# Stating every engine's instruction order for the attention and the first part of the first MLP

## The chip, the cores and the metric

The kernel runs on one core of one Trainium2 chip. The metric is device time in microseconds (us), the median of several runs; the output must agree with a float32 reference. The kernel is one program without loops at run time: every instruction of every engine is written out, and each engine works through its own list in order.

## What is computed

Attention with a causal mask and a linear memory term, for 4 batches, 8 heads, 576 positions and 64 values per head, then an MLP with squared ReLU (512 to 2048 to 512), then one with a softmax-weighted unit and a layer norm (512 to 1024 to 512), on 2304 tokens.

```
scores = scale * q @ k.T ; scores = where(causal, -1e9, scores)
a = exp(scores - max) ; a /= sum(a) + 1e-9 ; local = a @ v
q_p = elu(q) + 1 ; mem_out = (q_p @ M_prev) / (q_p . z_prev + 1e-6)
x = g * mem_out + (1 - g) * local          # g = sigmoid(beta), by head
r = max(x @ w_in, 0) ; y = (s * r * r + b) @ w_out
h = y @ w2_in ; solu = h * softmax(h) ; out = (layernorm(solu) * g_ln) @ w2_out
```

## The kernel before

**Units.** Attention goes through 16 units: 4 batches by 4 pairs of heads. The queries of a unit are cut into four chunks of 128 (index 0 to 3) and a tail of 64 for both heads (index 4). In the names of the rows the first number is the unit: s4_2 are the scores of unit 4, chunk 2; pr4_2_0 the probabilities of that chunk, head 0.

**A unit's chain.** `scores` (L329) multiplies on TensorE into ps_s, one pair of PSUM banks with a single buffer: one bank per head. Four groups follow each other there: chunks 0 and 1 together, 2, 3, and the tail (`tail_scores`, L360). VectorE adds the mask and takes the row maximum (L345, L363 for the tail), which also empties the banks for the next group. ScalarE takes the exponential (L312). TensorE transposes the result (L386, tiles pp), ScalarE copies it out of PSUM (L390, tiles pt), and `values` multiplies it by v (L421, and L424 for the tail, tiles po and pe). The memory term has its own transposes (L302 and L306) and products (L426, L427); the reciprocal sums are transposed at L292; VectorE writes the unit's result to xb (L428, L429).

**Matmul shapes.** The scores contract over 64 rows and two heads stand one above the other in the array; the row's form is 64\*128. The value products fill 64 columns each, two heads side by side; their form is 128\*64. All other matmuls use the whole array, 128\*128. In the trace each of these narrow float32 matmuls stands as two records, so x12 of L329 are six matmuls of the program.

**Filler.** `first_part` runs the first 4 of 16 column blocks of the first MLP on finished tokens between the attention's own matmuls (h: L440 to L442, y: L502 to L504), with its split of x (L469, L470) and its nonlinearity (L443, L450, L451, L454). `decode` turns float64 weights into two float32 parts: a load into one of three buffers raw (L154), then ScalarE (L159, L186) and VectorE (L160, L162, L164, L165, L187).

**What sets the order.** A scheduler of the framework puts the instructions of each engine in order when the program is built, from the order of the source and a timeline model of its own. The source steers it where it says that one instruction is to be issued after another: `exps` and `hidden` leave a mark, and `decode_to` (L197 to L202) asks that a decode step be issued after the last mark. The flag `attended` turns true once attention has been issued.

Of the kernel before, what the change touches and what calls it, by code (L numbers as in the profile page):

```python
# [17 lines left out]
P = 128  # L18
NEG = -8.0e9
FMAX = 3.0e38  # L20


@with_exitstack
def attention_mlp_kernel(
# [10 lines left out]
    B, NPAIR, _, NCH, _, D = q.shape  # L35
# [81 lines left out]
    order = [("in", f) for f in range(FP1)] + [("out", f) for f in range(FP1)]  # L117
# [50 lines left out]
    def decode(n):  # L168
        key = order[n]
        sc = None  # L170
        if key[0] == "in2" and key[2] >= 3:

            k = key[2]
            if k == 3:
                blk[3] = fetch(n)[0]
            d, x, y = ((0, 3, 0), (3, 2, 3), (2, 2, 0), (1, 1, 2))[k - 3]
            a = blk[d]
            nc.gpsimd.tensor_tensor(a, blk[x], blk[y], ALU.subtract)
        else:
            a, sc = fetch(n)  # L180
            if key[0] == "in2":
                blk[key[2]] = a
        pool = wpools[in_b(n)]
        w = pool.tile([P, 2, WN], F32R, tag="w", name=f"w{n}")
        if sc is None:
            nc.scalar.activation(w[:, 0], a, AF.Copy)  # L186
            nc.vector.tensor_tensor(w[:, 1], a, w[:, 0].bitcast(F32), ALU.subtract)  # L187
        else:
            nc.scalar.activation(w[:, 0], a, AF.Copy, scale=sc)
            nc.vector.scalar_tensor_tensor(w[:, 1], a, sc, w[:, 0].bitcast(F32), ALU.mult, ALU.subtract)  # L190
        wtiles[key] = w
# [4 lines left out]
    mark = [None]  # L196

    def decode_to(n):
        while decoded[0] < min(n, NW):
            with tc.issue_after(mark[0]) if mark[0] else nullcontext():  # L200
                decode(decoded[0])
            decoded[0] += 1  # L202

# [7 lines left out]
    class Attention:  # L211
# [102 lines left out]
        def scores(self, u, *cs):  # L314
# [23 lines left out]
            for i in cs:  # L338
                n = (i + 1) * P
                prs, mxs = [], []  # L340
                for j in range(2):
# [4 lines left out]
                                                   big[:, CF * P - i * P:CF * P - i * P + n],  # L346
                                                   -scale, FMAX, ALU.add, ALU.min, mx)
                    prs.append(pr)
# [3 lines left out]
        def tail_scores(self, u, ss):  # L352
# [5 lines left out]
            for t in range(2):  # L358
                cols = slice(t * HS, (t + 1) * HS)
                nc.tensor.matmul(ss[:, t, 0:HS], raw[:, QT:RL], raw[:, cols], start=True, stop=True)  # L360
                m0 = FMAX if t == 0 else mx
                mx = self.tiny.tile([P, 1], F32, tag="mx", name="mx")
# [71 lines left out]
    attended = [False]  # L434
# [39 lines left out]
    def first_part(k, pools):  # L474
# [13 lines left out]
        for f in range(FP1):  # L488
            h = ps[0].tile([P, 512], F32, tag="mh"[len(ps) - 1], name=f"h{k}_{f}")
            r, g = gtiles(f"{k}_{f}")  # L490
            decode_to(f + 1)
            hidden(wtiles["in", f], xh, xl, n, h[:, 0:n], r[:, 0:n], g[:, 0, 0:n], g[:, 1, 0:n])
            gq.append(g)
            yield
        for c in range(NC):
            pt = ps[-1].tile([P, 512], F32, tag="m", name=f"y{k}_{c}")
            o = pt[:, 0:n]
            decode_to(2 * FP1)
            for f in range(FP1):
                wc = [wtiles["out", f][:, t, c * P:(c + 1) * P] for t in range(2)]  # L500
                gh, gl = (gq[f][:, t, 0:n] for t in range(2))
                nc.tensor.matmul(o, wc[0], gh, start=(f == 0), stop=False)  # L502
                nc.tensor.matmul(o, wc[1], gh, start=False, stop=False)  # L503
                nc.tensor.matmul(o, wc[0], gl, start=False, stop=(f == FP1 - 1))  # L504
            y = ys.tile([P, NB], F32, tag="y", name=f"yo{k}_{c}")
            nc.scalar.activation(y[:, 0:n], o, AF.Copy)
            nc.sync.dma_start(yd[:, c, t0:t0 + n], y[:, 0:n])
            yield
# [27 lines left out]
    with ExitStack() as fctx:  # L536
# [7 lines left out]
        with ExitStack() as actx:  # L544
# [15 lines left out]
            for g in range(G + LAG):  # L560
                u, i = divmod(g, NS)
# [14 lines left out]
                if 0 <= g - LAG:  # L576
# [6 lines left out]
                    if li == CF:  # L583
                        at.values(lu)
                        at.load(lu + 2, "v")
                        if lu % NPAIR == NPAIR - 1:
                            filler.append(first_part(lu // NPAIR, fpools))
                decode_to(min(int(g / 3.4), RA))
                if filler and g >= FG:
                    debt += (B - 1) * (FP1 + NC) / (G - FG)  # L590
# [84 lines left out]
    def mlp2(mctx):  # L675
# [32 lines left out]
        def products(q, mxs):  # L708
# [6 lines left out]
            def product(o, form, k, more):  # L715
                yh, yl = form
                for i in range(KH):
                    w = wtiles["in2", i, k]
                    nc.tensor.matmul(o, yh[:, i], w[:, 0], start=(i == 0 and not more), stop=False,
                                     skip_group_check=True)  # L720
                    nc.tensor.matmul(o, yh[:, i], w[:, 1], start=False, stop=False, skip_group_check=True)
                    nc.tensor.matmul(o, yl[:, i], w[:, 0], start=False, stop=(i == KH - 1), skip_group_check=True)

            def leave(t, half, o, x, m0, m):
                nc.vector.tensor_tensor_reduce(hn[t][:, half * WN:(half + 1) * WN], o, x, -1.0, m0,
                                               ALU.add, ALU.min, m)
# [7 lines left out]
            product(W, fs1, 3, False)  # L734
            leave(1, 1, W, u3, FMAX, mxs[2])
            product(X, fa12, 1, True)
            leave(0, 0, X, big[:, 0:WN], FMAX, mxs[0])
            product(W, fs4, 2, True)
# [55 lines left out]

    with ExitStack() as mctx:
        mlp2(mctx)


_INS = ["z_prev", "beta", "moe_w_in", "moe_w_out", "moe_s", "moe_b", "moe2_w_in", "moe2_w_out", "moe2_g_ln"]
# [50 lines left out]
```

## Time and profile before

| what | us |
|---|---|
| median of 3 runs (849.80 to 850.04) | 849.98 |
| profiled execution, whole time | 849.68 |
| its span, first to last instruction | 847.5 |
| TensorE matmuls busy (PE) | 828.6 |
| TensorE weight loads busy (PEld) | 660.1 |
| VectorE busy (DVE) | 541.5 |
| ScalarE busy (ACT) | 550.6 |

The attention's last matmul starts at 305.5 us; the rest of the first MLP ends near 641 us, the second MLP fills the remainder. The granted TensorE clock is full (1.00, so the 2.4 GHz level) in all but the last stretch. Times are from the start of the span. A busy PE means that some matmul is in flight by the profile's model of their ends; a group's real price is the distance from its start to the start of the next group.

### The profile page before, as it was taken

The page shows a single profiled execution, that of the slowest core. Times are in us where ns is not written, and L with a number is a line of the kernel's source. Part 1 is how long each engine was busy: PE and PEld are TensorE (multiplying, and loading weights), DVE is VectorE, ACT ScalarE, POOL GpSimd, SP SyncE. Part 2 cuts the span into 40 slices and gives each one's busy share as a digit, 9 for nine tenths or more (in the row PEclk, how much of TensorE's full clock was granted, in tenths as well). Part 3 has the DMA queues.
Part 4 walks back from the last instruction along what each step waited for, and adds up shares of the span by engine and source line. Part 5 has one row for each costly group of instructions (what it writes and reads, how often), then busy time and mean ns, then how long its engine had stood idle before and what let it go on. Part 6 is the DMA issues. An engine that isn't in the chain of part 4 may idle for free.

```text
span 847.5 us, 13346 instructions
## 1 busy us (share of the span) xinstructions
PE 828.6 (98%) x4930; PEld 660.1 (78%) x4930; DVE 541.5 (64%) x1305; ACT 550.6 (65%) x1134; POOL 117.3 (14%) x124
## 2 busy tenths in 40 slices
PE   8999999999999999999999999999999999999997
PEld 6666776777677678888889888888887888888885
DVE  4989776968884747544556444473689666666552
ACT  5988787867876856665677666576785544444432
POOL 3122021101120200000000020020103333322000
PEclk9999999999999999999999999999999999999999
DMA  8344343534453013561223121121120000000001
GB/s 255 122 138 147 129 153 109 174 121 135 141 188 110 21 56 126 199 247 44 80 75 125 50 75 49 51 75 50 50 76 0 23 18 23 26 25 26 26 14 48
DMA packets 39759, 76.35 MB, mean 90 GB/s; under 512 B 6160, under 2 KB 16400, under 8 KB 39696
## 3 DMA queue, kind: packets, MB, share of 16 engines
q1 hardware_dynamic: 39696, 75.52, 26.8%
q8 instruction: 39, 0.64, 0.3%
q14 instruction: 24, 0.20, 0.1%
HBM read 61.35 MB, written 14.16 MB: 89 GB/s over the span
## 4 chain that ended last, share of the span: by engine, by line
PE 84%; DVE 8%; ACT 5%; issue 1%; DMA 1%; POOL 0%; SPq 0%; ACTq 0%; DVEq 0%; POOLq 0%
PE h L441 8%; PE h L440 8%; PE h L442 8%; PE y L646 6%; PE y L645 6%; PE y L647 6%; PE po L421 4%; PE o L779 4%; PE o L777 4%; PE o L778 4%; PE pp L386 3%; PE s L329 3%; PE y L502 2%; ACT pr L312 2%; PE y L503 2%; PE y L504 2%
## 5 line engine op out<-in xcount | busy, mean ns | idle before, releaser
L441 PE MATMUL h<-xl,w 128*128 128x512 f32 (+1 forms) x320 | 119.2, 373 | 0.4 <-DVE xl L470 0.4
L442 PE MATMUL h<-xh,w 128*128 128x512 f32 (+1 forms) x320 | 118.0, 369 | 0.0
L440 PE MATMUL h<-xh,w 128*128 128x512 f32 (+1 forms) x320 | 117.2, 376 | 0.4 <-ACT r L443 0.2
L443 ACT ACTIVATE r<-h 128x512 f32<-128x512 f32 (+1 forms) x80 | 43.1, 553 | 90.7 <-PE h L442 86.8
L448 DVE TENSOR_TENSOR g<-r,g 128x512 fp32r<-128x512 f32 (+1 forms) x60 | 39.6, 665 | 83.4 <-ACT r L447 83.4
L646 PE MATMUL y<-g,w 128*128 128x512 f32 (+1 forms) x240 | 87.2, 368 | 0.0
L645 PE MATMUL y<-g,w 128*128 128x512 f32 (+1 forms) x240 | 87.2, 368 | 0.0
L312 ACT ACTIVATE pr<-pr,mx 128x128 f32<-128x128 f32 (+3 forms) x128 | 70.9, 556 | 21.9 <-DVE mx L345 21.9
L390 ACT ACTIVATE pt<-pp,omg 128x128 f32<-128x128 f32 (+3 forms) x128 | 61.1, 522 | 19.4 <-PE pp L386 19.3
L441 PEld LDWEIGHTS h<-xl,w 128*128 128x128 f32 x320 | 60.4, 189 | 12.1 <-DVE xl L470 1.9
L440 PEld LDWEIGHTS h<-xh,w 128*128 128x128 f32 x320 | 59.5, 189 | 11.0 <-ACT r L443 1.3
L442 PEld LDWEIGHTS h<-xh,w 128*128 128x128 f32 x320 | 60.4, 189 | 9.7
L647 PE MATMUL y<-g,w 128*128 128x512 f32 (+1 forms) x240 | 67.6, 368 | 0.0
L345 DVE CUSTOM_DVE_ANT_0 pr<-s,big 128x128 f32<-128x128 f32 (+3 forms) x128 | 56.4, 485 | 15.0 <-PE s L329 14.8
L779 PE MATMUL o<-w,zl 128*128 128x512 f32 x144 | 56.6, 393 | 0.8 <-DVE var L755 0.8
L777 PE MATMUL o<-w,zh 128*128 128x512 f32 x144 | 56.7, 394 | 0.3 <-ACT zh L771 0.3
L778 PE MATMUL o<-w,zh 128*128 128x512 f32 x144 | 56.1, 390 | 0.0
L329 PEld LDWEIGHTS s<-kq 64*128 64x128 f32 x640 | 40.3, 188 | 18.8 <-issue 9.8
L421 PE MATMUL po<-pt,v 128*64 128x256 f32 (+1 forms) x384 | 54.2, 355 | 0.7 <-ACT pt L390 0.7
L329 PE MATMUL s<-kq 64*128 64x128 f32 x640 | 49.9, 289 | 2.8 <-DVE mx L345 2.6
L646 PEld LDWEIGHTS y<-g,w 128*128 128x128 f32 x240 | 45.3, 189 | 7.5
L645 PEld LDWEIGHTS y<-g,w 128*128 128x128 f32 x240 | 45.3, 189 | 7.5
(165 smaller groups left out, 1862.8 us busy)
## 6 DMA issues: line engine op xcount, KB each, us to landing
raw<-in_moe_w_in_dram SPq DMA_DIRECT2D x24, 512.0 KB, 3.7
raw<-in_moe_w_out_dram SPq DMA_DIRECT2D x24, 512.0 KB, 3.3
kq<-in_kq_dram SPq DMA_DIRECT2D x16, 608.0 KB, 4.0
xr<-xd SPq DMA_DIRECT2D x8, 1024.0 KB, 5.5
q<-in_q_dram SPq DMA_DIRECT2D x16, 320.0 KB, 3.6
v<-in_v_dram SPq DMA_DIRECT2D x16, 320.0 KB, 3.2
xd<-xb SPq DMA_DIRECT2D x4, 1152.0 KB, 5.9
out_dram<-os SPq DMA_DIRECT2D x18, 256.0 KB, 2.0
```

The lines of the kernel that those rows point to most:

```text
L312: mark[0] = nc.scalar.activation(pr, pr, AF.Exp, bias=mx, scale=-1.0, accum_out=sm).ins
L329: self.last = nc.tensor.matmul(ss[:, j, c0 + k * P:c0 + (k + 1) * P], x[:, S + i * P:S + (i + 1) * P], x[:, k * P:(k + 1) * P], start=True ...
L421: nc.tensor.matmul(o, vr[:, c, j], m, start=(cp == 0 and c == 0), stop=False)
L440: nc.tensor.matmul(ps, wc[0], xh[:, c, 0:n], start=(c == 0), stop=False)
L441: nc.tensor.matmul(ps, wc[0], xl[:, c, 0:n], start=False, stop=False)
L442: nc.tensor.matmul(ps, wc[1], xh[:, c, 0:n], start=False, stop=(c == NC - 1))
L645: nc.tensor.matmul(o, wc[0], gh[:, 0:n], start=(f == fs[0]), stop=False)
L646: nc.tensor.matmul(o, wc[1], gh[:, 0:n], start=False, stop=False)
L647: nc.tensor.matmul(o, wc[0], gl[:, 0:n], start=False, stop=(f == fs[-1]))
L777: nc.tensor.matmul(oo, zh, w[:, 0], start=(f == 0), stop=False)
L778: nc.tensor.matmul(oo, zh, w[:, 1], start=False, stop=False)
L779: nc.tensor.matmul(oo, zl, w[:, 0], start=False, stop=(f == NF2 - 1))
```

## The change

The program gets a table `ORDER` with one list of runs per engine (a+n stands for n consecutive instructions from the a-th, counted as the source issues them), and `state_order`, called last, which ties each instruction to the one before it in that list. The lists reach through the attention and the first part of the first MLP; what follows is left to the scheduler. In `decode_to` the request to issue after the last mark now holds only once `attended` is true. No instruction is added to or taken from the computation, and no tile changes. Lines below the table stand 92 further on: L421 of the new program is L329 of the old, L513 is L421.

```diff
+ORDER = {
+    "PE": """
+0+30 46 34+6 47 40 62+4 41+5 30+4 68+3 48+8 71+3 56+6 102+3 66 80+7 67 87 105+2 74+6 107+7 88 92+5 89+3 126+6 97 101
...
+    "Activation": """
+0 2+2 5 4 8+2 6+2 1 16 12+2 17 10+2 24 15 25 14 20 18 21+3 27 26 31 28+3 34 128 36 32+2 38+2 37 42 19 48 40 43 49 41
...
+}
+
+def state_order(tc):
+    traced = {}
+    for i in tc.nc.cur_bb.bb.instructions:
+        traced.setdefault(str(i.engine).split(".")[-1], []).append(i)
+    info = mybir.DependencyInfo(mybir.DependencyClass.NoSync, mybir.DependencyReason.DATA)
+    for engine, runs in ORDER.items():
+        seq = []
+        for run in runs.split():
+            a, _, n = run.partition("+")
+            seq += traced[engine][int(a):int(a) + int(n or 1)]
+        for x, y in zip(seq, seq[1:]):
+            tc.add_manual_dep(y, x.name, info, reason="order")
...
-            with tc.issue_after(mark[0]) if mark[0] else nullcontext():
+            with tc.issue_after(mark[0]) if mark[0] and attended[0] else nullcontext():
...
     with ExitStack() as mctx:
         mlp2(mctx)
+    state_order(tc)
```

**First place, TensorE, from the values of unit 3 to the third score group of unit 4.** Before:

```order
L421 MATMUL po3_990<-pt3_1_916,v3_619 64x256 x6
L421 MATMUL po3_990<-pt3_1_916,v3_619 64x128 x2
L329 MATMUL s4_0_927<-kq4_701 128x128 x6
L292 MATMUL tr3_964<-ident_58,r3_912 128x128 x4
L302 MATMUL tp3_972<-ident_58,ph3_839 128x128 x4
L306 MATMUL tq3_978<-ident_58,ph3_839 128x128
L329 MATMUL s4_2_1032<-kq4_701 128x128 x6
L386 MATMUL pp3_8_981<-ident_58,pr3_t_896 128x128 x4
```

Now, at the same place:

```order
L478 MATMUL pp3_7_958<-ident_58,pr3_3_1_877 128x128 x4
L513 MATMUL po3_990<-pt3_0_848,v3_619 64x256
L421 MATMUL s4_0_927<-kq4_701 128x128 x6
L384 MATMUL tr3_964<-ident_58,r3_912 128x128 x4
L394 MATMUL tp3_972<-ident_58,ph3_839 128x128 x4
L398 MATMUL tq3_978<-ident_58,ph3_839 128x128
L513 MATMUL po3_990<-pt3_0_848,v3_619 64x256
L513 MATMUL po3_990<-pt3_0_848,v3_619 64x128 x2
L513 MATMUL po3_990<-pt3_1_916,v3_619 64x256 x6
L421 MATMUL s4_2_1032<-kq4_701 128x128 x6
```

The value products of unit 3 (po3) stood ahead of the first scores of unit 4; most of them now stand between s4_0 and s4_2, behind the nine transposes tr3, tp3, tq3.

**Second place, TensorE, the value products of unit 4 on the tiles of its first two chunks (pt4_0).** Before:

```order
L421 MATMUL po4_1224<-pt4_0_1056,v4_822 64x256
L386 MATMUL pp4_5_1115<-ident_58,pr4_2_1_1042 128x128 x3
L386 MATMUL pp4_6_1156<-ident_58,pr4_3_0_1071 128x128 x4
L421 MATMUL po4_1224<-pt4_0_1056,v4_822 64x256
L421 MATMUL po4_1224<-pt4_0_1056,v4_822 64x128 x2
L360 MATMUL s4_4_1088<-kq4_701 128x288
L386 MATMUL pp4_7_1162<-ident_58,pr4_3_1_1074 128x128 x4
```

Now:

```order
L421 MATMUL s5_0_1131<-kq5_908 128x128 x6
L513 MATMUL po4_1224<-pt4_0_1056,v4_822 64x256 x2
L513 MATMUL po4_1224<-pt4_0_1056,v4_822 64x128 x2
L519 MATMUL pe3_991<-mq3_971,Mb0_133 128x64
L394 MATMUL tp4_1176<-ident_58,ph4_1047 128x128
L398 MATMUL tq4_1182<-ident_58,ph4_1047 128x128
L421 MATMUL s5_2_1254<-kq5_908 128x128 x6
```

Before, one product stood alone between transposes and three others came two transposes' groups later; now the four stand together, directly behind the scores s5_0.

**Third place, VectorE, the two maxima of the third score group of unit 5.** (The row mx is the second half of a maximum, which hands out the result.) Before:

```order
L345 ISA pr5_3_0_1312,mx_1313<-s5_3_1303,big_63 128x512
L345 ISA mx_1313 128x1
L345 ISA pr5_3_1_1315,mx_1316<-s5_3_1303,big_63 128x512
L345 ISA mx_1316 128x1
L363 ISA pr5_t_1341,mx_1343<-s5_4_1340,big_63 128x288
```

Now:

```order
L437 ISA pr5_3_0_1312,mx_1313<-s5_3_1303,big_63 128x512
L437 ISA mx_1313 128x1
L546 SCALAR_TENSOR_TENSOR g0_2_1428<-r0_2_1427,b_sb_80,g0_2_1428 128x512
L353 SCALAR_TENSOR_TENSOR ph5_1269<-q5_882,ph5_1269 128x640
L252 TENSOR_SCALAR wa8_1486<-wa8_1486 128x512
L437 ISA pr5_3_1_1315,mx_1316<-s5_3_1303,big_63 128x512
L437 ISA mx_1316 128x1
```

The two maxima followed each other; now a step of the MLP's nonlinearity (g0_2), one of the memory term (ph5) and one of a weight's decode (wa8) stand between them.

## Rows read from the trace of the kernel before

**Rows 1.** The page, part 1: engine, busy us (share of the span), instructions.

```profile
PE 828.6 (98%) x4930; PEld 660.1 (78%) x4930; DVE 541.5 (64%) x1305; ACT 550.6 (65%) x1134; POOL 117.3 (14%) x124
```

**Rows 2.** Busy time by stretch: bounds, length, each engine's us (instructions), clock, DMA.

```profile
0.00:15.00 15.00, 12.52 (x98) 9.03 (x99) 6.97 (x29) 8.15 (x23) 5.71 (x17) 1.00 0.80 233
15.00:305.50 290.50, 281.96 (x2247) 204.55 (x2245) 224.08 (x671) 228.27 (x567) 47.78 (x45) 1.00 0.40 130
...
350.00:847.50 497.50, 489.89 (x2352) 408.60 (x2350) 282.77 (x555) 288.36 (x497) 63.76 (x62) 1.00 0.17 59
```

**Rows 3.** Waits of PE from 15 to 305.5 us: total us, times, longest.

```profile
PE s L329 <- DVE mx L345: 2.6, 4, 1.3
PE s L360 <- DVE mx L345: 1.6, 3, 1.2
PE pe L424 <- ACT ptl L396: 1.3, 4, 0.4
```

**Rows 4.** Timeline of PE from 36 us: start, length, instruction, count [idle before].

```profile
37.49 0.60 PE L302 MATMUL tp<-ident,ph 128*128 128x128 f32 x4
37.93 0.27 PE L306 MATMUL tq<-ident,ph 128*128 128x128 f32 x1
38.13 0.94 PE L329 MATMUL s<-kq 64*128 64x128 f32 x12
39.00 0.66 PE L386 MATMUL pp<-ident,pr_t 128*128 128x128 f32 x4
...
41.31 1.16 PE L329 MATMUL s<-kq 64*128 64x128 f32 x16
42.41 0.80 PE L424 MATMUL pe<-ptl,v 128*64 128x64 f32 x20
```

**Rows 5.** The same view at two groups of value products, 46.94 and 91.01 us.

```profile
46.94 0.65 PE L421 MATMUL po<-pt,v 128*64 128x256 f32 x2
47.51 0.50 PE L441 MATMUL h<-xl,w 128*128 128x512 f32 x1
...
91.01 1.73 PE L421 MATMUL po<-pt,v 128*64 128x256 f32 x16
92.67 0.50 PE L441 MATMUL h<-xl,w 128*128 128x512 f32 x1
```

**Rows 6.** Timeline of all engines around the longest wait, units 3 and 4.

```profile
68.73 0.94 PE L329 MATMUL s<-kq 64*128 64x128 f32 x12
...
70.29 0.58 DVE L369 TENSOR_SCALAR pr_t<-pr_t,sm,gmt 128x576 f32<-128x576 f32 x1
...
70.53 0.27 PE L306 MATMUL tq<-ident,ph 128*128 128x128 f32 x1
70.78 0.28 DVE L345 CUSTOM_DVE_ANT_0 pr<-s,big 128x128 f32<-128x128 f32 x1
...
72.12 0.94 PE L329 MATMUL s<-kq 64*128 64x128 f32 x12 [1.32 <-DVE mx L345]
```

**Rows 7.** Groups of DVE, 15 to 305.5 us: busy us, mean ns | idle before.

```profile
L165 DVE TENSOR_TENSOR wa<-wa,raw 128x512 f32<-128x512 f32 x18 | 14.0, 776 | 0.1
...
L261 DVE SCALAR_TENSOR_TENSOR ph<-q,ph 128x640 f32<-128x640 f32 x15 | 12.3, 819 | 1.3 <-ACT ph L260 1.3
L267 DVE TENSOR_REDUCE den<-q 128x10 f32<-128x640 f32 x15 | 12.1, 809 | 0.1
L454 DVE SCALAR_TENSOR_TENSOR g<-r,b_sb,g 128x512 fp32r<-128x512 f32 x12 | 11.2, 932 | 2.3 <-ACT g L451 2.3
...
L470 DVE TENSOR_TENSOR xl<-xb,xh 128x512 fp32r<-128x512 f32 (+3 forms) x15 | 10.6, 710 | 1.0 <-ACT xh L469 1.0
L160 DVE TENSOR_SCALAR wa<-wa 128x512 int32<-128x512 int32 x18 | 10.2, 565 | 0.5 <-ACT wa L159 0.2
...
L369 DVE TENSOR_SCALAR pr_t<-pr_t,sm,gmt 128x576 f32<-128x576 f32 x16 | 9.3, 579 | 0.5
```

**Rows 8.** The page, part 6: a DMA issue by line, KB each, us to landing.

```profile
raw<-in_moe_w_in_dram SPq DMA_DIRECT2D x24, 512.0 KB, 3.7
```

More of the change, by code (lines that the diff above doesn't have):

```diff
@@ L20 @@
 FMAX = 3.0e38
+ORDER = {
+    "PE": """
[26 rows of a table added]
+""",
+    "Activation": """
[15 rows of a table added]
+""",
+    "DVE": """
[16 rows of a table added]
+""",
+    "Pool": """
+3 15 17 5 11 0 13 2 6 12 8 10 14 16 20 18+2 23 21+2 26 24+2 29 27 32 28 30 35 31 33+2 38 36+2 41 39+2 44 42+2 47
+45+2 50 48+2 53 51+2 56 54+2 59 57+2 60+2
+""",
+    "SP": """
[3 rows of a table added]
+""",
+}
[11 more added lines that the diff above has]
+            tc.add_manual_dep(y, x.name, info, reason="order")
 @with_exitstack
```

58 rows, old and new, of the table ORDER are left out of this document.

## The prediction

> **What bounds the kernel now.** I read the busy times first. TensorE has a matmul in flight for 828.6 of 847.5 us [rows 1], no other engine passes 65%: the end is set by TensorE, and the question is how much of its time is work. The second view is the busy time by stretch [rows 2]. Behind 350 us TensorE idles 7.6 us of 497.5, and the table reaches only a little past the attention; I take that part as unchanged. Everything is decided in the stretch from 15 to 305.5 us. There PE is idle for 290.5 - 281.96 = 8.5 us; VectorE is busy 224 us (77%) and ScalarE 228 us (79%), so neither is the bound, but both work through their lists in order and are close enough to hold TensorE up for a moment. The third view, the waits of PE in that stretch, says what they are held up for: mostly the row maxima that empty the score banks (2.6 us and 1.6 us), then the copy of a transposed tile [rows 3].
>
> The idle time is not all that an order can change. In the timeline, a price is read from start to start. Twelve scores take 39.00 - 38.13 = 0.87 us, sixteen take 42.41 - 41.31 = 1.10 us [rows 4]: four more cost 0.23, twelve are worth 0.69, and 0.18 us is paid once when TensorE leaves a group of scores. It is paid equally when the next group has the whole array (the first pair) and when it has the narrow columns (the second). On the way in, the single transpose at 37.93 holds TensorE for 38.13 - 37.93 = 0.20 us, where the four before it took 0.44, or 0.11 each [rows 4]: 0.09 us for entering a narrow shape from the full one. For value products, a lone one (two records, 256 columns) takes 47.51 - 46.94 = 0.57 us, and a group of eight (six of 256 columns, two of 128, the two heads always in turn) takes 92.67 - 91.01 = 1.66 [rows 5]. If a pair of heads runs side by side for p and leaving costs e, then a lone product is p + e, the eight are 3.5 p + e; so p = 0.44 and e = 0.13 us. A product without its partner beside it so wastes half a pair, 0.22 us at 256 columns and, by the same ratio, 0.11 at 128. None of this shows as idle: the 98% hides it.
>
> **The change, part by part.** The work is the same, instruction for instruction; only places in line differ. I counted the groups in both orders up to the first matmul of the fourth token block (h3_0), that is, the whole attention.
>
> Leaving a group of scores: 51 times before, 48 now, at 0.18 us: 0.5 us. Leaving a group of value products: 69 times before, 51 now, at 0.13: 2.3 us. Entering a narrow shape from the full one: 92 times before, 61 now, at 0.09: 2.8 us. The second place of the order shows how: po4 stood in two pieces between transposes, now it stands whole and directly behind s5_0, where the shape is narrow already. Sum 5.6 us. Value products without a partner: 15 of 256 columns and 19 of 128 before, 7 and 9 now: 8 x 0.22 + 10 x 0.11 = 2.9 us. Together 8.5 us. These are prices TensorE pays itself; no other engine's work hides them, and TensorE is the bound, so they come off the end if nothing else becomes late. Bounds: none of them, if TensorE then waits for the others (below), and all of them.
>
> The waits: 8.5 us of idle after 15 us. The longest, 1.32 us, is the third score group of unit 4 [rows 6]. The scores at 68.73 are followed by nine transposes that end their issue with the one at 70.53; VectorE starts on the first of four maxima only at 70.78, behind the tail of unit 3, and the banks are free at 72.12. The first place of the order now puts nine value products between: seven of 256 and two of 128 columns, 4 x 0.44 + 0.13 = 1.9 us. That covers 1.32. At four more of the waits that I could place (the copies before po5 and po15, one tail group of unit 11, the memory term of unit 1) the matmuls between giver and taker grow by 0.4 to 3.1 us by the same prices; I book some 3 us in all as removed. The other side: between the tail's scores and the next unit's first scores there stood about 2.1 us of matmuls in units 0, 3 and 10 and now stand 1.0 to 1.2, between s7_2 and s7_3 2.8 became 1.5, and the wait of pe for its copied tile has no more cover than before in units 6, 7 and 15. I book 3 us as added, which is the mean of a known wait, 4.2 us in 7 cases for the score banks [rows 3], or 0.6, at five places. So net nothing; from -8.5 (all waits gone) to the price of the second rival.
>
> The request to issue a decode step after the last exponential goes. It held no data back: in the new lists every place is stated, so it costs nothing by itself. What matters is that decode steps stand elsewhere. SyncE's list, which issues the loads, is the same as before through the 22nd load of weights, while ScalarE reads some raw tiles earlier (the fifth within unit 2 and not 3, three in a row in unit 6). A load lands 3.7 us after its issue [rows 8], and at worst ScalarE waits that long once or twice for one; TensorE would see what its own queue does not cover. I take zero, with up to 3.7 us for the range, the price of one uncovered landing; below zero it can't go, since an early read gives nothing to TensorE. The first 15 us hold 2.5 us of idle [rows 2] for the first loads and the first maxima, which both orders need; one small instruction (omg) now stands behind the first maxima instead of ahead, worth 0.2 us at most, and I leave it out.
>
> Sum, against the profiled execution's 849.7 us: 849.7 - 8.5 = 841.2. That execution stands 0.3 below the median of its runs, so 841.5 for a median.
>
> **A rule that says otherwise.** By the rows, weight loads fill 204.55 of 290.5 us in the attention (70%), and 408.60 of 497.5 behind 350 us (82%) [rows 2]. The Trainium skill's page "Trainium Kernel Development and Optimization", section "Best Practices", asks to judge TensorE's distance from its limit by the arithmetic done and by the share of weight loads, and not by matmul busy time. The trace agrees that busy hides something. By that measure the attention would have room to 290.5 x 70/82 = 248 us, 42 us less, and the kernel would go to 807. The rows leave no such time: 99 groups of narrow matmuls still have to be left (48 x 0.18 + 51 x 0.13 = 15 us), and 61 entered (5 us). I give it one chance in a hundred.
>
> **The rivals.** *The waits go as well.* If every taker stands behind enough matmuls, the 8.5 us of idle go too: 841.5 - 8.5 = 833. For it: the first place, and neither VectorE nor ScalarE is the bound. Against it: five places got tighter, and VectorE and ScalarE do the same work in less time (77 and 79% become 79 and 81% over 282 us), so their queues are less forgiving.
>
> *VectorE's list delays the score banks, and the kernel is slower.* Before, the maxima of each of the 48 groups of chunks stood together, but for three short instructions in all. Now 17 other instructions stand between them, in ten groups; the third place of the order is one. Eleven of the 17 are long: three of L470 (0.71 us), two of L261 (0.82), two of L160 (0.57), one each of L165 (0.78), L267 (0.81), L369 (0.58) and L454 (0.93) [rows 7]: 8.0 us. Between the two maxima of a tail stand 73 instructions, 54 before; 19 more at VectorE's mean of 224.08/671 = 0.33 us [rows 2] are 6.3. The next scores write the banks only when the last of these maxima is done, and every matmul behind them in TensorE's list stands still with them; ScalarE's exponential, too, comes later. Were all of it exposed: 841.5 + 14.3 = 856. It decides against the change once more than 8.5 + 1.7 = 10.2 of the 14.3 us shows on TensorE. Against it: at the third place s5_3 and s5_4 now have 3.8 us of matmuls between them, where 2.8 stood, so the 2.3 us inserted there find some cover; behind s1_0, where four instructions came in, 2.1 became 3.1.
>
> *It comes out even.* The same mechanism at half its price: the long insertions alone, 8.0 us, would take back nearly all of the 8.5, and the time stays within 848.3 to 851.7. That the table does nothing can be excluded, since the lists of both programs differ.
>
> **How the numbers follow.** The forecast (waits unchanged within some 4 us) 0.50, at 841.5, itself 837 to 845.5. The waits gone as well, 829 to 837: 0.19; the weight-load rule 0.01. Part of the gain lost, 845.5 to 848.3: 0.07. Even: 0.07. Slower through VectorE's list: 0.16. About 0.2%, 1.7 us, is what a measurement of this kernel can tell from no change. So faster is 0.50 + 0.19 + 0.01 + 0.07 = 0.77, same 0.07, slower 0.16. The range should leave out no more than 2 in 10: from 831, a little under the rival of vanished waits (0.05 below), to 852, which takes in the forecast with a landing and the even case, and leaves 0.13 above.
>
> **What would show it.** In the new profile the attention's last matmul starts near 297 us (305.5 - 8.5), and the time behind it is as before. Groups of L421 (now L513) stand mostly in fours, eights and more, and the same matmuls have shorter distances. PE's idle time between 15 us and the end of the attention is 8 to 9 us: if it falls to 3 the first rival holds, if it rises above 15 with waits of scores for maxima, the second. The wait at s4_2 is gone. The prediction would be wrong in its sum if the price of leaving a narrow shape were no constant but a wait in disguise, which shows as fewer groups at unchanged time with no more idle.

## The result, and the profile after

The changed kernel takes 829.27 us (829.06 to 829.67, four runs) against 850.01 beside it: a ratio of 0.9757 [0.974, 0.9773], 20.7 us less. The profiled execution took 829.67 us with a span of 827.5, at full granted clock. The forecast was 841.5, the range ended at 831: the direction was right, the gain more than twice what was summed. One profiled execution among the experiments took 1153.06 us at a mean granted clock of 0.65 and is left out of the times below; all others stand at 0.979 or more.

The page's first part, the same columns as [rows 1]:

```profile
PE 814.1 (98%) x4930; PEld 656.9 (79%) x4930; DVE 533.7 (64%) x1305; ACT 551.9 (67%) x1134; POOL 117.2 (14%) x124
```

TensorE's busy share is 98%, as it was, and yet 20 us are gone. The last product of the memory term, which ends the attention, is found in the view of its line (duration least/median/most in ns, then the first and the last start):

```profile
L519 PE MATMUL pe<-mq,Mb x32: 217/275/323, 26.5 to 286.0; 128*128 128x64 f32 x32
```

It starts at 286.0 where it was 305.5, 19.5 us earlier. What is behind it takes 827.5 - 286.0 = 541.5 us, 542.1 before. So 19.5 of the 20 us of the span lie in the attention. The stretches, to be held against [rows 2] (bounds, length, busy us and instructions of PE, PEld, DVE, ACT, POOL, clock, DMA share, GB/s):

```profile
0.00:15.00 15.00, 11.81 (x98) 8.71 (x98) 5.79 (x26) 8.22 (x24) 5.51 (x17) 1.00 0.78 236
15.00:286.00 271.00, 268.36 (x2246) 201.89 (x2246) 217.56 (x673) 229.50 (x567) 47.91 (x46) 1.00 0.42 139
330.00:827.50 497.50, 489.89 (x2351) 408.46 (x2349) 283.81 (x557) 288.51 (x496) 63.81 (x62) 1.00 0.17 58
```

PE is idle for 271.00 - 268.36 = 2.6 us of the middle stretch (8.5 before) and for 3.2 of the first (2.5 before): 5.2 us less. PE's busy time in the last stretch is the same to the hundredth of a microsecond. So 14 of the 19.5 us came out of time in which PE shows as busy. The waits that are left, as in [rows 3]:

```profile
PE tr L384 <- ACT r L374: 0.7, 1, 0.7
PE pe L516 <- ACT ptl L488: 0.6, 1, 0.6
PE s L421 <- DVE mx L437: 0.5, 2, 0.3
PE s L452 <- DVE xb L521: 0.3, 1, 0.3
PE s L452 <- DVE mx L437: 0.2, 1, 0.2
```

The waits of scores for the maxima of chunks were 2.6 + 1.6 us in 7 cases; they are 0.5 + 0.2 in 3. The longest wait now, 0.7 us, is a new one: at 282.06 the last unit's reciprocal sums come late. The longest of before, 1.32 us ahead of s4_2 [rows 6], stood at the first place of the order. PE's timeline there now:

```profile
62.71 0.27 PE L398 MATMUL tq<-ident,ph 128*128 128x128 f32 x1
62.91 2.16 PE L513 MATMUL po<-pt,v 128*64 128x256 f32 x18
65.00 0.94 PE L421 MATMUL s<-kq 64*128 64x128 f32 x12
65.87 0.33 PE L478 MATMUL pp<-ident,pr_t 128*128 128x128 f32 x1
66.04 0.27 PE L490 MATMUL ppu<-ident,pr_t 128*128 128x128 f32 x1
66.15 0.49 PE L478 MATMUL pp<-ident,pr_t 128*128 128x128 f32 x3
66.57 0.44 PE L513 MATMUL po<-pt,v 128*64 128x128 f32 x4
```

The scores at 65.00 have no wait: the value products from 62.91 stand in it. The same rows show a price that the sum lacked. Five transposes stand between the scores and the next value products, from 65.87 to 66.57: 0.70 us, where five at 0.11 are 0.55. The first costs 66.04 - 65.87 = 0.17 us, the second, which follows a full-array matmul, 66.15 - 66.04 = 0.11, the last three 0.42 instead of 0.33. So besides 0.09 on the way into the narrow shape there is 0.06 in the first matmul back in the whole array, together 0.15.

To see all such prices I took the distance from each matmul's start to the next and subtracted the steady step of its shape, which is the distance inside a long group. The steps add up to 241.3 us in each program; what is left over, up to the end of the attention, falls from 63.1 to 43.7. Idle time is part of it and stands in columns of its own. By what the run was:

| run of matmuls | before: runs, us over | of it idle | after: runs, us over | of it idle |
|---|---|---|---|---|
| full array, up to the next narrow one | 92, 29.9 | 8.5 | 61, 19.6 | 3.3 |
| scores | 51, 13.0 | 1.2 | 48, 11.2 | 0.6 |
| value products (po and pe counted apart; left 69 and 51 times) | 69, 20.2 | 0.2 | 58, 12.9 | 0.8 |

Without the idle time, full-array runs cost 5.1 us less, scores 1.2 and value products 7.9; the idle time falls by 5.2. The totals depend on what is taken for a steady step. The differences do not, since both programs hold the same matmuls. The price of one full-array run is cleanest in the runs that hold 128-column transposes alone and no wait: 0.15 us over 0.109 each, the median of 19 such runs before and of 13 now.

Value products cost more before than a count of lone ones tells. A group of the program before:

```profile
109.02 1.73 PE L421 MATMUL po<-pt,v 128*64 128x256 f32 x14
110.68 0.66 PE L292 MATMUL tr<-ident,r 128*128 128x128 f32 x4
```

Its seven products (five of 256 columns, two of 128) take 1.66 us, as long as the eight of [rows 5]. The starts of the single matmuls show that a 256-column product runs beside a 128-column one there, and the group loses 0.21 us. Before, 14 groups were of this kind (nine of these seven products, five of three); now three are left that stand by themselves. And three groups of eight took 2.0 to 2.2 us in the order before (the first from 17.39 to 19.55 us) where the eight of [rows 5] take 1.66; the new order has none of them.

### The profile page after: what moved, and what is told of

It is laid out like the page before. It is cut to its first block, busy times and chain, and to the rows that moved or that the text cites. A ratio compares the mean times of both kernels' runs of the same rounds, so it can differ in the third digit from the quotient of the medians.

```text
span 827.5 us, 13276 instructions
## 1 busy us (share of the span) xinstructions
PE 814.1 (98%) x4930; PEld 656.9 (79%) x4930; DVE 533.7 (64%) x1305; ACT 551.9 (67%) x1134; POOL 117.2 (14%) x124
## 4 chain that ended last, share of the span: by engine, by line
PE 91%; DVE 4%; ACT 2%; DMA 1%; POOL 1%; issue 1%; SPq 0%; DVEq 0%; POOLq 0%
PE h L532 8%; PE h L533 8%; PE h L534 8%; PE y L738 6%; PE y L739 6%; PE y L737 6%; PE pp L478 5%; PE s L421 5%; PE o L871 4%; PE o L869 4%; PE o L870 4%; PE po L513 4%; PE y L596 2%; PE y L594 2%; PE y L595 2%; PE s L452 2%
## 5 line engine op out<-in xcount | busy, mean ns | idle before, releaser
L404 ACT ACTIVATE pr<-pr,mx 128x512 f32<-128x512 f32 (+3 forms) x128 | 70.8, 555 | 16.1 <-DVE mx L437 15.6
L533 PEld LDWEIGHTS h<-xl,w 128*128 128x128 f32 x320 | 60.3, 189 | 10.8 <-DVE xl L562 1.1
L437 DVE CUSTOM_DVE_ANT_0 pr<-s,big 128x128 f32<-128x128 f32 (+3 forms) x128 | 57.1, 487 | 14.5 <-PE s L421 12.6
L482 ACT ACTIVATE pt<-pp,omg 128x512 f32<-128x512 f32 (+3 forms) x128 | 60.1, 524 | 7.8 <-PE pp L478 7.3
L421 PEld LDWEIGHTS s<-kq 64*128 64x128 f32 x640 | 39.7, 187 | 14.5 <-issue 7.2
L478 PE MATMUL pp<-ident,pr 128*128 128x128 f32 x320 | 48.8, 276 | 2.2 <-ACT pr L404 2.1
L421 PE MATMUL s<-kq 64*128 64x128 f32 x640 | 48.6, 287 | 0.8 <-DVE mx L437 0.5
```

The costliest lines, as they stand in the source:

```text
L404: mark[0] = nc.scalar.activation(pr, pr, AF.Exp, bias=mx, scale=-1.0, accum_out=sm).ins
L421: self.last = nc.tensor.matmul(ss[:, j, c0 + k * P:c0 + (k + 1) * P], x[:, S + i * P:S + (i + 1) * P], x[:, k * P:(k + 1) * P], start=True ...
L478: nc.tensor.transpose(pp[:, e * n + c * P:e * n + (c + 1) * P], pr[:, c * P:(c + 1) * P], ident)
L533: nc.tensor.matmul(ps, wc[0], xl[:, c, 0:n], start=False, stop=False)
```

## The experiments

Each is the changed kernel with another table or without a part of it. Where a table differs, the edit is shown as instructions in their order, and not as the table's numbers. Times of before beside them were 849.7 to 850.2.

**The statement without the order.** The table holds the order of before, for all engines.

```diff
 ORDER = {
     "PE": """
-... (the new places)
+... (the places of before)
```

> The table of the new kernel, filled with the order that the kernel before has on every engine, and the edit of decode_to as in the new kernel. If the gain comes from where instructions stand, this is the kernel before again: 850 us, within 1 us, with 305 us to the attention's end. If stating an order were itself worth something (other semaphores, fewer waits written into the program), it would be below 845.

Measured 850.04, ratio 0.9995 [0.9986, 1.0004]. To state an order costs and gives nothing; neither do the edit of `decode_to` and the removed request when every place is stated. The gain is in the order.

**The edit of `decode_to` alone.**

```diff
-            with tc.issue_after(mark[0]) if mark[0] else nullcontext():
+            with tc.issue_after(mark[0]) if mark[0] and attended[0] else nullcontext():
```

> The kernel before with the edit of decode_to alone and no table: the framework's scheduler orders everything, with decode steps no longer tied to the last exponential. If the gain comes from the table, this lies within 4 us of 850. If the freed decode steps were the cause, it would be near 830.

Measured 877.68, 1.0318 [1.0298, 1.0338]: 27 us slower. Without table or request the scheduler sets decode steps ahead of what TensorE waits for: between 50 and 100 us VectorE runs 9 to 11 of each decode step, 4 before, and ScalarE idles 9.7 us there for raw tiles. Two of its waits, and two stretches:

```profile
PE tr L292 <- ACT r L282: 8.1, 3, 4.3
PE s L329 <- DVE mx L345: 5.8, 6, 1.8
...
50.00:100.00 50.00, 39.22 (x276) 26.82 (x276) 44.85 (x122) 37.21 (x93) 6.87 (x6) 0.84 0.48 158
150.00:300.00 150.00, 149.40 (x1172) 111.36 (x1170) 89.06 (x294) 109.67 (x274) 22.25 (x23) 1.00 0.33 107
```

Between 50 and 100 us VectorE is busy for 44.85 of 50, PE idles 10.8, and the granted clock is 0.84 there, while it is full again after 150 us.

**Part of the lists.** TensorE's list alone; all lists but TensorE's; TensorE's alone with `decode_to` as before.

```diff
 ORDER = {
     "PE": """
...
-    "Activation": """
-    "DVE": """
-    "Pool": """
-    "SP": """
```

> The new kernel with only TensorE's list stated; the scheduler orders the other four engines around it. If most of the gain is TensorE's own price of changing shape (fewer groups of narrow matmuls), that part stays and only waits return: 830 to 840 us, and the same sum of start-to-start excess outside waits. If the gain came from VectorE's and ScalarE's lists, 845 to 850.

> The new kernel without TensorE's list; the lists of the other four engines stay stated. If most of the gain is TensorE's own price, the scheduler's TensorE order decides it: 842 to 852 us, if it cuts the narrow groups as before. If the lists of the others bring the gain, near 830.

> TensorE's list of the new kernel alone, with decode_to as before, so that decode steps stay tied to the last exponential and the scheduler orders the other engines. If the loss of the kernel with TensorE's list alone (885.7) came from the edit of decode_to, as its own loss of 27 us suggests: 835 to 855. If TensorE's list needs the other lists whatever the mark does: above 865.

Measured 885.66 (1.0408 [1.0388, 1.0429]), 874.25 (1.0275 [1.0258, 1.0292]) and 865.5 (1.0182 [1.0168, 1.0196]). Each part by itself is slower than before; PE idles 37.5, 23.5 and 26.3 us after 15 us. The first two contain the edit of `decode_to`, which took 877.68 without any list: against that, TensorE's list alone loses 8.0 us and the other lists alone gain 3.4. With `decode_to` as before, TensorE's list alone loses 15.7 us against the kernel before. In the second program TensorE has the new orders of its partners and an order of its own that the scheduler makes:

```profile
PE po L485 <- ACT pt L454: 4.3, 5, 2.8
PE s L424 <- DVE mx L409: 2.6, 2, 1.6
PE pp L450 <- ACT pt L454: 2.6, 6, 0.7
```

The lists are one plan. What one list is worth can't be read by leaving out the others, since the scheduler then fills the gap with a third order. Joining one engine's old list to another's new one was not tried: the two contradict each other at tiles that both engines hand on.

**Shapes alone.** The order of before, stated, with the pieces of each group of value products gathered at the place of the last one: entries from the full array 92 to 79, leavings of value products 69 to 51, products without a partner 34 to none.

```diff
-MATMUL po4<-pt4_0,v4 64x256
 MATMUL pp4_5<-ident,pr4_2_1 128x128 x3
 MATMUL pp4_6<-ident,pr4_3_0 128x128 x4
-MATMUL po4<-pt4_0,v4 64x256
+MATMUL po4<-pt4_0,v4 64x256 x2
 MATMUL po4<-pt4_0,v4 64x128 x2
```

> The kernel before with its own order stated on every engine (850), but on TensorE each split group of value products (L421) is gathered at the place of its last piece; nothing else moves. Lone products go from 34 to none, leaving the narrow columns from 69 times to 51, entering a narrow shape from 92 to 79. By the prices of the prediction: 15 x 0.22 + 19 x 0.11 + 18 x 0.13 + 13 x 0.09 = 8.9 us, so 841, if no wait grows. If coming back to the whole array costs another 0.1 us that the prediction did not count: 10 us, 840. If the prices were waits in disguise: 850.

Measured 843.64, 0.9931 [0.9918, 0.9945]: 6.2 us off with a change of shapes only. In its trace the time over the steady steps falls by 4.2 us, although PE's idle time grows by 5.4: hidden under busy, 9.5 us went. That execution took 845.49 us, with a granted clock of 0.66 between 10 and 15 us. The profiled execution of the stated order of before (851.5) had the same clock there, so the two can be compared: idle time grows by 4.5, 10.6 us go under busy, and the net 6.1 is what the medians show. By the prices of the prediction the part under busy should be 13 x 0.09 + 18 x 0.13 + 15 x 0.22 + 19 x 0.11 = 8.9. The waits that ate the rest:

```profile
PE s L414 <- DVE mx L430: 5.2, 8, 1.3
PE pe L509 <- ACT ptl L481: 1.7, 4, 0.7
```

**More entries.** The new order with a transpose or an MLP product moved so that 20 more runs of the full array stand between narrow ones: entries 61 to 81, leavings as they were.

```diff
-MATMUL pp3_7<-ident,pr3_3_1 128x128 x4
+MATMUL pp3_7<-ident,pr3_3_1 128x128 x3
 MATMUL po3<-pt3_0,v3 64x256
+MATMUL pp3_7<-ident,pr3_3_1 128x128
 MATMUL s4_0<-kq4 128x128 x6
```

> The new kernel, with one matmul of the whole array (13 times of the MLP, 7 times a transpose) moved by one group, to stand between two narrow groups that followed each other: entries to a narrow shape from 61 to 81, nothing else. At 0.09 us each, as in the prediction: +1.8 us, 831.1. At 0.2 us, as the distances in the new trace suggest: +4, 833.3. If shapes had no price: 829.3.

Measured 835.82 (833.69 to 837.9), 0.9834 [0.9818, 0.985]. In the profiled execution (833.69) the attention ends 4.0 us later, with 0.6 us more idle: 3.4 us for 20 runs, 0.17 each and not 0.09. The other three runs took 835.09 to 837.9, two of them at a mean clock of 0.997 and 0.995; no trace shows what they add, so 0.17 rests on the fastest run.

**VectorE's insertions.** The 17 instructions that the new order puts between maxima of a score group moved behind them.

```diff
 ISA pr4_1_0,mx<-s4_0,big 128x256
 ISA mx 128x1
-TENSOR_SCALAR sm<-sm 128x1
 ISA pr4_1_1,mx<-s4_0,big 128x256
 ISA mx 128x1
+TENSOR_SCALAR sm<-sm 128x1
```

> The new kernel, with the 17 instructions that stand between the maxima of one score group on VectorE moved behind the group's last maximum. If they find cover where they stand (no wait of the new trace is charged to them), within 1 us of 829.3. If they delay the score banks, as the second rival had it, faster by up to the 3 us of idle that is left, 826 to 828.

Measured 831.86 (0.979 [0.9777, 0.9804]): 2.6 us slower than with them. The second rival had them delay the score banks; taken away, PE idles 4.6 us after 15 us instead of 2.6:

```profile
PE h L533 <- DVE xl L562: 1.1, 2, 0.7
PE s L452 <- DVE mx L455: 0.9, 1, 0.9
```

One kind of the inserted steps, xl, is what TensorE needed next: late, it costs 1.1 us. The other new waits were not traced to a single step.

**Cover taken back.** Cover is the matmuls that stand between an instruction that another engine waits for and the next one that waits for that engine. In units 3, 5, 10, 11, 12 and 14 the value products go back ahead of the score group that they follow in the new order. By the counts this program is even a little better: leavings of value products 51 to 48, products without a partner 16 to 12.

```diff
 MATMUL po3<-pt3_0,v3 64x256
+MATMUL po3<-pt3_0,v3 64x256
+MATMUL po3<-pt3_0,v3 64x128 x2
+MATMUL po3<-pt3_1,v3 64x256 x6
 MATMUL s4_0<-kq4 128x128 x6
 MATMUL tr3<-ident,r3 128x128 x4
...
-MATMUL po3<-pt3_0,v3 64x256
-MATMUL po3<-pt3_0,v3 64x128 x2
-MATMUL po3<-pt3_1,v3 64x256 x6
 MATMUL s4_2<-kq4 128x128 x6
```

> The new kernel, with the value products of units 3, 5, 10, 11, 12 and 14 that stand between two score groups of the next unit put ahead of the first of the two, where the kernel before had them: 1 to 2 us less of matmuls between those groups, slightly fewer shape changes (-1.2 us). If the waits went because each taker stands behind enough matmuls: waits of scores for maxima return at these six places, 0.5 to 1.3 us each, 831 to 835. If they went because of VectorE's and ScalarE's lists alone: 828.

> The same kernel as the one before with six groups of value products put back, whose profiled execution was disturbed. The runs beside it took 837.7 to 839.1. If the loss is waits of scores for maxima at the six places: PE's idle behind 15 us rises from 2.6 to 8 us or more, most of it charged to the maxima or to the copies of pt that the earlier products need, and the attention ends near 294 us. If it is the price of shapes, idle stays near 3.

Both are the same kernel. Measured 838.43 (0.9867 [0.9852, 0.9882]) and 837.37 (0.9856 [0.9828, 0.9885]): 8.1 us lost against the new order in the second, whose rows follow. The attention ends 7.9 us later, and PE idles 5.4 us more. The other 2.5 us show as busy, and no run separates prices from short waits in them. The first place of the order:

```profile
64.92 0.94 PE L421 MATMUL s<-kq 64*128 64x128 f32 x12 [0.32 <-DVE mx L437]
66.88 0.30 PE L478 MATMUL pp<-ident,pr_t 128*128 128x128 f32 x1 [1.01 <-DVE pr_t L461]
```

0.32 + 1.01 = 1.33 us where the program before waited 1.32. Further waits follow the moved products of units 10, 11, 12 and 14; the last, on all engines:

```profile
273.72 1.03 PE L513 MATMUL po<-pt,v 128*64 128x256 f32 x8
...
274.68 0.94 PE L421 MATMUL s<-kq 64*128 64x128 f32 x12
275.67 0.29 DVE L437 CUSTOM_DVE_ANT_0 pr<-s,big 128x128 f32<-128x128 f32 x1 [2.27 <-PE s L421]
...
277.01 0.94 PE L421 MATMUL s<-kq 64*128 64x128 f32 x12 [1.39 <-DVE mx L437]
```

VectorE sat idle for 2.27 us until it got the scores, because value products stood ahead of them; then TensorE sat idle for 1.39 until VectorE had emptied the banks. In the new order, at the same place, the scores start at 266.55 us, the products follow from 267.42 to 269.08, and the next scores start there with no wait before them: the same work fills both waits. The view of VectorE's maxima of chunks gives the sum: time for which VectorE idled until scores came (us, times), in before, in the new order and in this program:

```profile
  PE s L329: 14.8, 15
```

```profile
  PE s L421: 12.6, 16
```

```profile
  PE s L421: 21.6, 18
```

**Still fewer pieces.** The new order, every group of value products whole, at the place of its last piece, and at that of its first.

```diff
-MATMUL po2<-pt2_0,v2 64x256
 MATMUL s2_4<-kq2 128x288
...
-MATMUL po2<-pt2_0,v2 64x256
+MATMUL po2<-pt2_0,v2 64x256 x2
 MATMUL po2<-pt2_0,v2 64x128 x2
```

> The new kernel, with each split group of value products gathered at the place of its last piece, as in the merged kernel before: lone products from 16 to none (7 x 0.22 + 9 x 0.11 = 2.5 us), 4 groups and 3 entries fewer (1 us). If nothing waits for the delayed products: 826. If half is given back in waits, as it was there: 827.5. If the plan has no slack, 830 or more.

> The same, but gathered at the place of the first piece: 2.5 us less for lone products and 1.5 for groups, against waits for the copies of the transposed tiles, which the later pieces need. 825.5 if these are ready, 830 or more if TensorE waits 0.5 us for them at ten places.

Measured 833.73 (0.9812 [0.9798, 0.9825]) and 836.12 (0.9835 [0.9821, 0.9848]). Value products do get cheaper, and waits take more than that back: PE idles 7.2 and 9.8 us after 15 us. In the first, the clock was 0.96 from 280 to 285 us and 0.70 in the next five, by which I estimate 5 x 0.04 + 5 x 0.30 = 1.7 of its 4.5 us. The first and the second program's main waits:

```profile
PE tr L384 <- ACT r L374: 2.2, 1, 2.2
PE pp L478 <- DVE pr_t L461: 1.9, 2, 1.3
```

```profile
PE s L421 <- DVE mx L437: 3.4, 5, 1.4
PE po L513 <- ACT pt L482: 1.7, 3, 0.7
```

No variant was faster than the changed kernel.

## Why the prediction was right in its direction and short in its size

*The place and the kind of gain* held. TensorE is the bound, the stretch behind the attention hardly moved, and most of the gain came out of busy time, by fewer and fuller groups. "The price a wait in disguise" can be excluded as the whole: time moved with shapes alone (the gathered order of before, and the 20 added entries).

*Leaving a narrow shape, and lone products* (0.5 + 2.3 + 2.9 = 5.7 us) had the right mechanism and too small a size: without waits it was 1.2 us for scores and 7.9 for value products. The gathered order of before agrees, with 10.6 us under busy for 8.9 by the prices. The sum gave an uneven group 0.11 us for its one product without a partner, but the group loses 0.21, and it held no price for the groups of eight that took 2.0 to 2.2 us.

*Entering a narrow shape from the full array* was mis-sized: 0.09 us was read from the last full matmul ahead of a narrow one, and the first full matmul behind one pays as well. Together they are 0.15 by the runs of transposes alone, and 0.17 by the 20 added ones. Instead of 2.8 us the 31 runs fewer gave 5.1, or 0.165 each. The gathered order of before gives less, 1.1 us for 13 runs fewer, with waits grown around them. The Trainium skill's page "TensorEngine Tiling (Array Packing)", section "Key Properties", says that changing the tiling mode drains TensorE; the rows agree that each change has its price, in both directions, and give the price that the page doesn't state.

*The waits* were the step that failed. 3 us were booked as removed, 3 as added, net nothing; measured is 5.2 us less idle. What was booked as removed came: the wait at s4_2 is gone, and moving the products back returns it at nearly its size. What was booked as added did not. Of the places that got tighter one shows a wait, the 0.6 us of pe for ptl in unit 7, and that has another cause (below); the 0.7 us of the last unit stand at a place that was not on the list. At the tail of unit 10, one of the three with half the cover, PE's rows and VectorE's read:

```profile
192.41 0.65 PE L452 MATMUL s<-kq 128*128 128x288 f32 x2
192.90 0.95 PE L478 MATMUL pp<-ident,pr 128*128 128x128 f32 x7
193.10 0.52 DVE L455 CUSTOM_DVE_ANT_0 pr_t<-s,mtail,mx 128x288 f32<-128x288 f32 x1 [0.54 <-PE s L452]
193.78 0.94 PE L421 MATMUL s<-kq 64*128 64x128 f32 x12
```

VectorE had been idle for 0.54 us when the scores came and took its maximum at once; the 0.9 us of transposes are just enough cover for the next scores. I compared cover with cover and gave each loss the mean of a known wait, without asking whether VectorE would still be busy with something else at that place. This one place shows it standing ready; for the others the rows show only that no wait came. Over the whole attention VectorE idles less for scores, for those of chunks (12.6 us, 14.8 before) and most of all for tails:

```profile
DVE pr_t L363 <- PE s L360: 19.1, 12, 3.2
```

```profile
DVE pr_t L455 <- PE s L452: 7.0, 10, 1.6
```

Part of that may follow from the shorter time itself, so it does not prove the cause. With the six groups moved back the tails stay at 6.9, and only the chunks lose.

*The request in `decode_to`* "costs nothing by itself" holds with the lists stated; alone the edit costs 27 us. The moved decode steps were the open term: one load did come late, as the bound of 3.7 us allowed. In unit 7 ScalarE waits 2.20 us for a raw tile, the copy ptl stands behind that step in its list, and pe waits for ptl (timeline of ScalarE, then of PE):

```profile
139.98 0.69 ACT L251 ACTIVATE wa<-raw 128x512 f32<-128x512 f32 x1 [2.20 <-DMA raw<-in_moe_w_in_dram]
140.58 0.57 ACT L488 ACTIVATE ptl<-pp 128x512 f32<-128x512 f32 x1
...
141.20 0.80 PE L516 MATMUL pe<-ptl,v 128*64 128x64 f32 x20 [0.59 <-ACT ptl L488]
```

It is the only wait for a raw tile, and of its 2.20 us 0.59 reach TensorE: zero was a little low. So the one tight place that shows a wait owes it to the load, by these rows; it was not tested by a run of its own.

*The rivals.* Most of the waits vanished (833, given 0.19), on top of the forecast and not in its place, and with the larger prices of shapes the time fell below that rival's own. VectorE's list as a delay is refuted: moving the insertions behind the maxima costs 2.6 us, of which 2.0 show as idle. The rival of the weight loads would have given 807 with loads at 82%; they went from 70 to 201.89 of 271.00 us, 74%. The Trainium skill's page "Trainium Kernel Development and Optimization", section "Best Practices", warns against judging by the matmul busy share. The trace agrees: it read 98% before and after.

*The sum again:* 8.5 us were booked, and up to the end of the attention 19.4 came. They are 5.2 us of idle time (nothing booked), 5.1 for full-array runs (2.8 booked), 7.9 for value products (5.2 booked) and 1.2 for scores (0.5 booked). Waits shorter than the modelled end of the matmul ahead would not show as idle, and no run separates them from prices. How the 5.2 us divide between TensorE's list and those of its partners is open too: six groups moved back show that cover in TensorE's list is worth as much (5.4), not that the other lists add nothing.

*The range* was too short at its lower end because it set the forecast and the vanished waits as either-or, and took the prices of shapes as exact.

## What to carry to other kernels

Read the price of a change of shape on both sides, in the last matmul ahead of it and in the first behind it, and count runs, since the busy share shows none of it. Time a group with a product left over as a whole: it can lose more than the half pair. Put the matmuls that another engine waits for first and those that nobody waits for behind them, so that the same work fills both waits; before booking a wait for a place that got tighter, look whether the engine it waits for is idle there. A stated order is a plan for all engines: half of one can be worse than none.

## What the runs showed of the hardware beyond that

Stretches with much idle time on TensorE came with a lower clock. In the program with TensorE's list alone, PE was busy for 26.06 of 35 us and then 36.30 of 50, and the clock granted was 0.76 and 0.83, a mix of the 2.4 and the 1.2 GHz level:

```profile
15.00:50.00 35.00, 26.06 (x164) 17.71 (x163) 31.73 (x85) 23.64 (x54) 4.83 (x4) 0.76 0.61 191
50.00:100.00 50.00, 36.30 (x246) 26.30 (x247) 45.78 (x119) 35.33 (x83) 6.00 (x5) 0.83 0.47 150
```

In before and in the changed kernel, with 97% and more of the stretch behind 15 us busy, it was full there. Between 10 and 15 us the profiled executions differ. The clock was 0.66 there in three of them (the stated order of before, its gathered order, the maxima put together), though PE was busy for all 5 us, and full in before and in the changed kernel. In the 5 us before that, PE was busy for 2.98, 3.16 and 2.38 us in the three, and for 2.87 in the changed kernel, whose clock stayed full; so these rows do not say when it falls. In the gathered order, the execution with the lower clock took 845.49 us, the three others 843.41 to 843.66.
